# Three regroupings in a two-stage kernel: an earlier half of w_out, groups that share a wait, products moved ahead of block 2

## The chip, the cores and the metric

The kernel runs on one core of a Trainium2 chip. The metric is the device time of one execution in microseconds. The median of seven executions counts, and less is better.

## The reference

The first half is a normalised linear attention over 8 batches of 8 heads, 576 rows and 64 columns. The second half is a two-layer network with a leaky activation over all 4608 rows.

```python
kv  = einsum('bhsd,bhse->bhde', k, v)          # per head, 64 x 64
out = einsum('bhsd,bhde->bhse', q, kv)
x   = out / sqrt(mean(out*out, -1) + 1e-6) * g_norm
x   = x.transpose(0, 2, 1, 3).reshape(4608, 512)
h   = x @ w_in                                 # 512 -> 2048
g   = maximum(h, 0) + alpha * minimum(h, 0)
y   = g @ w_out                                # 2048 -> 512, float32
```

## The kernel before

The 4608 rows are cut into nine blocks (`w` = 0 to 8) of 512. For each block the first layer makes 16 groups (`g`) of 128 features. A group is four matmuls (`m1_mm`), one for each of four pairs of heads, which sum into one PSUM bank. `m1_evac` then empties that bank: ScalarE writes `m_sb`, and VectorE makes `gt` out of `m_sb` and the bank. The second layer is the y products (`y_mm`): each of the four row tiles (`a`) of a block sums 16 products, one per group, into a bank, and `y_out` copies that bank and stores it. A product reads `gt` of its group and one 128-row block of `w_out`.

Nothing is scheduled by the compiler. All five engines run in the order in which the code issues to them (`manual_schedule`), so a line of code that is moved is moved on every queue that it issues to. The eight PSUM banks are named by pools: `H_POOL` (h0 to h2), `ps_s` ("s"), `ps_y` ("y") and `ps_o` (o0 to o2). A new tile of a name waits until the last reader of the old one is done.

Loads from memory are issued by GpSimd, on one queue, in the order of the code. `load_rest` (L190) issues the four quarters of `w_in`, two quarters of `w_out`, then k, q and v of batch 1, then the other two quarters of `w_out` (L197). Each `load` is two transfers. Transposes by DMA and the stores of results are issued on the queue of SyncE (SP).

Blocks 0 and 1 take their input from batches 0 and 1 by way of TensorE: `step_t` transposes q, `step_kv` makes kv of the batch, `step_ot` multiplies both for a pair and ends with a square on ScalarE (or VectorE), `ssq_mm` sums the squares by a matmul and takes Ln and Exp on ScalarE, and `norm` writes the input `xt` of that pair on VectorE. For block 1 these steps stand between the y products of block 0, which `ahead` issues by hand, one group of four tiles at a time (`ya` to `yd`, L623 to L668). `ssq_mm` of all four pairs of block 1 uses the bank "s" (`S_POOL`). The regroup of batch 2's q, a VectorE copy, stands between the norms of pairs 2 and 3; behind it SP issues the transpose that makes `qtm`.

From block 2 on the input `xm` comes another way. `tile_a` multiplies a tile of rows and squares it, `tile_b` and `tile_c` make its scale, `tile_d` writes the scaled rows, and SP transposes them into `xm`. `phase_steps` lays these out as steps, one per group of the block before. The rows that are left over of batch 1 come by `step_tail_ot`, `step_tail_ssq` and `tail_norm`.

In the main loop (L676) each group of block `w` is followed by y products. In block 1 they are block 1's own, of tile 0, two groups behind; later blocks issue those of the block before, and block 2 also what is left of block 1. Two small copies on GpSimd (`gate`) hold the loads of batch 3 back: the first waits for `qtm` of batch 2, the second for `xm` of block 2.

Of the kernel before, what the change touches and what calls it, by code (L numbers as in the profile page):

```python
# [9 lines left out]
FP32 = mybir.dt.float32  # L10
FP16 = mybir.dt.float16
# [6 lines left out]
def kernel(  # L18
# [14 lines left out]
    N_TOK, D_MODEL = out.shape  # L33
    D_FF = moe_w_in.shape[1]

    P = 128
    NPAIR = H // 2
    W = 512
    NW = N_TOK // W
    TPW = W // P  # L40
# [4 lines left out]
    NF = D_FF // P  # L45
    NC = D_MODEL // P
    assert NC == NPAIR and 0 < REM < P
    inv_d = 1.0 / D
    NB_PE = 2

    const_p = ctx.enter_context(tc.tile_pool(name="constp", bufs=1))
    w_p = ctx.enter_context(tc.tile_pool(name="weights", bufs=1))
# [20 lines left out]
            name=nc.get_next_instruction_name(),  # L73
# [33 lines left out]
    def load(b, nm, h0=0, h1=H):  # L107
        load_part(b, nm, True, h0, h1)
        load_part(b, nm, False, h0, h1)
# [50 lines left out]
    WQ = 4  # L160
    w_in_sb = []
    w_out_sb = []
    FW = D_FF // WQ
    GW = NF // WQ
# [6 lines left out]
        )  # L171
        w_in_sb.append(t)

    def load_w_out(i):
        t = w_p.tile([P, GW, D_MODEL], FP16, name=f"w_out_sb{i}")
        nc.gpsimd.dma_start(
            out=t[:],
            in_=moe_w_out[i * GW * P : (i + 1) * GW * P, :].rearrange("(g p) m -> p g m", p=P),
        )
        w_out_sb.append(t)  # L180

    def w_in_blk(c, g):
        i, r = divmod(g, GW)
        return w_in_sb[i][:, c, r * P : (r + 1) * P]

    def w_out_blk(g):
        i, r = divmod(g, GW)
        return w_out_sb[i][:, r, :]

    def load_rest():  # L190
        for i in range(WQ):
            load_w_in(i)
        load_w_out(0)
        load_w_out(1)
        for nm in "kqv":
            load(1, nm)
        for i in range(2, WQ):  # L197
            load_w_out(i)


    warm_ps = ps_y.tile([P, W], FP32, name="warm_ps", tag="y")
# [209 lines left out]
    def tile_b(b, t):  # L411
        n, _, sq = tiles[b, t]
        ss = attn_p.tile([P, H], FP32, name="ss", bufs=3)
        nc.vector.tensor_reduce(  # L414
            out=ss[0:n], in_=sq[0:n], op=ALU.add, axis=mybir.AxisListType.X,
        )
        tiles[b, t][2] = ss
# [14 lines left out]
    def tile_d(b, t):  # L432
        n, ot_ps, rg = tiles.pop((b, t))
        x = attn_p.tile([P, H, D], FP16, name="xrow", bufs=3)
        nc.vector.tensor_mul(out=x[0:n], in0=ot_ps[0:n], in1=rg[0:n])  # L435
        i = 0
        while i < n:
            w, c = divmod(b * S + t * P + i, W)
            m = min(n - i, W - c)
            nc.sync.dma_start_transpose(  # L440
                out=xm(w)[:, :, c : c + m], in_=x[i : i + m].rearrange("p h d -> p (h d)"),
            )
            i += m

    def phase_steps(w):


        if w >= NW:
            return []
        todo = [(b, t) for b in range(NB_PE, min(B, w + 1)) for t in range(NT)  # L450
                if (b, t) not in done and b * S + t * P < (w + 1) * W]
        done.update(todo)
        steps = []

        kv_at = {NB_PE: 3, NB_PE + 1: 6, NB_PE + 2: 2}.get(w, 0)
        n = {NB_PE: 4, NB_PE + 1: 2}.get(w, 0)
        steps += [([], [], []) for i in range(n)]

        lags = (0, 1, 4) if w == NB_PE else (0, 1, 2)
        if w == NB_PE:  # L460
            todo = [x for t in todo for x in (t, None)][:-1]
        if w in (NB_PE + 1, NB_PE + 2):
            k = [b for b, t in todo].index(w)
            todo[k:k] = [None] * (3 if w == NB_PE + 1 else 1)
        for i in range(len(todo) + lags[2]):
            a, b, d = (
                [todo[i - k]] if 0 <= i - k < len(todo) and todo[i - k] else [] for k in lags
            )
            begin = [lambda x=x: tile_b(*x) for x in b] + [lambda x=x: tile_d(*x) for x in d]
            mid = [lambda x=x: tile_c(*x) for x in b]  # L470
            end = [lambda x=x: tile_a(*x) for x in a]
            steps.append((begin, mid, end))
        if w < B:
            steps[kv_at][2 if w == NB_PE else 1].append(lambda: step_kv(w, pool=next_o() if kv_at else (ps_s, "s")))
        return steps
# [5 lines left out]
    H_POOL = [(ps_h, f"h{i}") for i in range(3)]  # L481

    def m1_mm(h_ps, w, g, cs, cols=slice(0, W)):
        for c in cs:
            nc.tensor.matmul(  # L485
                out=h_ps[:, cols], lhsT=w_in_blk(c, g), rhs=xt_of(w, c)[:, cols],
                start=(c == 0), stop=(c == NC - 1 and cols.stop == W),
            )
# [13 lines left out]
    def m1_group(w, g, pool=None):  # L502
        if pool is None:
            pool = H_POOL[n_group[0] % 3]
            n_group[0] += 1
        h_ps = pool[0].tile([P, W], FP32, name="h_ps", tag=pool[1])
        m1_mm(h_ps, w, g, range(NC))
        m1_evac(h_ps, w, g)


    def y_mm(y, w, a, g, cols=slice(0, D_MODEL)):
        nc.tensor.matmul(  # L512
            out=y[:], lhsT=gts[w, g][:, a * P : (a + 1) * P], rhs=w_out_blk(g)[:, cols],
            start=(g == 0), stop=(g == NF - 1),
        )
# [107 lines left out]
    def ahead(g0, g1, tiles=range(TPW)):  # L623
        for g in range(g0, g1):
            for a in tiles:
                y_mm(ys[a], 0, a, g)
# [3 lines left out]
    QW = NF - GW  # L630
    regroup(1, "k")
    ahead(0, 3)
    regroup(1, "q")
    ahead(3, 6)
    step_t(1, 0, S_POOL)
    step_t(1, 1, O1, nc.scalar)
    step_t(1, 2, H_POOL[0])
    step_t(1, 3, H_POOL[1], nc.scalar)
    ahead(6, 7)
    step_kv(1, pool=S_POOL)  # L640
    ahead(7, 8)
    step_ot(1, 0, H_POOL[0])
    step_ot(1, 1, O1)
    step_ot(1, 2, H_POOL[1], nc.vector)
    ahead(8, 9, range(2))
    ssq_mm(1, 0, S_POOL)
    ahead(8, 9, range(2, TPW))
    ahead(9, 10)
    ssq_mm(1, 1, S_POOL)
    norm(1, 0)  # L650
    ahead(10, 11)
    step_ot(1, 3, H_POOL[0])
    norm(1, 1)
    ssq_mm(1, 2, S_POOL)
    ahead(11, QW)
    ahead(QW, NF, (0,))
    ssq_mm(1, 3, S_POOL)
    norm(1, 2)
    regroup(2, "q")
    transpose_q(2)  # L660
    y_out(ys[0], 0, 0)
    ahead(QW, NF, (1,))
    norm(1, 3)
    ahead(QW, NF, (2,))
    y_out(ys[1], 0, 1, nc.vector)
# [6 lines left out]

    LOAD_G = 6
    n_group[0] = 1
    AHEAD = NF - 2
    for w in range(1, NW):  # L676
        steps = phase_steps(w + 1)
        for g in range(NF):
            if g == LOAD_G and 4 < w + 2 < B:
                load_batch(w + 2)  # L680
            if w == 1:
                parts = [(0, g - NF + AHEAD)] if g >= NF - AHEAD else []
            else:
                n0 = AHEAD if w == 2 else 0

                n1, d = TPW * NF - n0, 2 * (w == 2)
                cut = lambda i: max(0, (n1 + d) * i // NF - d)
                parts = [divmod(n0 + i, NF) for i in range(cut(g), cut(g + 1))]
            begin, mid, end = steps.pop(0) if steps else ([], [], [])
            for f in begin:  # L690
                f()
            m1_group(w, g, [H_POOL[1], S_POOL, H_POOL[2], H_POOL[0]][g % 4] if w == 1 else None)
            for f in mid:
                f()
            for a, gg in parts:
                if gg == 0:
                    pool, tag = ((ps_y, "y"), (ps_s, "s"))[a % 2]
                    y = pool.tile([P, W], FP32, name="y_ps", tag=tag)
                wy = w if w == 1 else w - 1
                y_mm(y, wy, a, gg)  # L700
                if gg == NF - 1:
                    y_out(y, wy, a)
            for f in end:
                f()
            if (w, g) == (1, 9):
                step_tail_ot(0, next_o())
            if (w, g) == (1, 11):
                step_tail_ssq(0, next_o())
            if (w, g) == (1, 13):
                tail_norm(0)  # L710
            if (w, g) == (1, 0):
                regroup(2, "k", eng=nc.gpsimd)
            if (w, g) == (1, 2):


                gate = const_p.tile([1, 1], FP16, name="gate")
                nc.gpsimd.tensor_copy(out=gate[:], in_=qtms[2][0:1, 0, 0:1])
                load(3, "q")
                load(3, "k")
            if (w, g) == (1, 9):  # L720
                regroup(3, "q", eng=nc.gpsimd)
            if (w, g) == (1, 12):

                nc.gpsimd.tensor_copy(out=gate[:], in_=xm(2)[0:1, 0, W - 1 : W])
                load(3, "v")
                transpose_q(3)
                regroup(3, "k", eng=nc.gpsimd)
            for i in {5: (0, 1), 6: (2, 3), 7: (4,), 8: (5,)}.get(g, ()) if w == 2 else ():
                load_part(4, "qkv"[i // 2], i % 2 == 0)
            if w > 1 and g == LOAD_G + 3 + 3 * (w == 2) and w + 2 < B:  # L730
                regroup_batch(w + 2)
            if w > 1 and g == NF - 3 and w + 2 < B:
                transpose_q(w + 2)
# [43 lines left out]
```

## Time and profile before

| | |
|---|---|
| median of 7 executions | 291.58 us (291.37 to 291.88) |
| profiled execution | 291.47 us, span 289.5 us |
| TensorE matmul busy | 280.7 us (97% of the span), 1545 matmuls |
| TensorE weight load busy | 138.6 us (48%) |
| VectorE busy | 165.8 us (57%) |
| ScalarE busy | 154.4 us (53%) |
| GpSimd busy | 99.2 us (34%) |
| mean DMA rate | 123 GB/s |

The profiled execution's time is 2.0 us more than its span. A row of the profile names the engine, the line of the kernel, what is written and read, the shape and the count, then busy time and mean duration. Engines are PE (TensorE matmul), PEld (its weight loads), DVE (VectorE), ACT (ScalarE), POOL (GpSimd) and SP (SyncE). Matmuls overlap: a row gives the latency of each, while PE takes the next one after a shorter step, which can be read from two start times.

### The profile page before, as it was taken

The page shows a single profiled execution, that of the slowest core. Times are in us where ns is not written, and L with a number is a line of the kernel's source. Part 1 is how long each engine was busy: PE and PEld are TensorE (multiplying, and loading weights), DVE is VectorE, ACT ScalarE, POOL GpSimd, SP SyncE. Part 2 cuts the span into 40 slices and gives each one's busy share as a digit, 9 for nine tenths or more (in the row PEclk, how much of TensorE's full clock was granted, in tenths as well). Part 3 has the DMA queues.
Part 4 walks back from the last instruction along what each step waited for, and adds up shares of the span by engine and source line. Part 5 has one row for each costly group of instructions (what it writes and reads, how often), then busy time and mean ns, then how long its engine had stood idle before and what let it go on. Part 6 is the DMA issues. An engine that isn't in the chain of part 4 may idle for free.

```text
span 289.5 us, 4268 instructions
## 1 busy us (share of the span) xinstructions
PE 280.7 (97%) x1545; PEld 138.6 (48%) x1545; DVE 165.8 (57%) x256; ACT 154.4 (53%) x300; POOL 99.2 (34%) x109
## 2 busy tenths in 40 slices
PE   5899999999999999999999999999999999999994
PEld 1544464554454554455445544554445444444443
DVE  4448846698777576448744864478448644444300
ACT  1298438587665664448543844486448544444220
POOL 8822330555658237504842474243004100000000
PEclk9999999999999999999999999999999999999999
DMA  7999999999899837971899189815212312121133
GB/s 90 198 206 206 198 204 198 187 210 169 137 154 180 177 65 98 208 178 39 122 207 199 30 132 209 163 31 93 45 36 57 82 38 48 45 47 43 39 72 72
DMA packets 66196, 35.54 MB, mean 123 GB/s; under 512 B 32752, under 2 KB 61696, under 8 KB 66176
## 3 DMA queue, kind: packets, MB, share of 16 engines
q0 software_dynamic: 29632, 18.35, 45.3%
q1 hardware_dynamic: 36384, 16.80, 29.1%
q8 instruction: 12, 0.20, 0.3%
q10 hardware_dynamic: 160, 0.13, 0.2%
q14 instruction: 8, 0.07, 0.1%
HBM read 36.71 MB, written 9.44 MB: 159 GB/s over the span
## 4 chain that ended last, share of the span: by engine, by line
PE 93%; DMA 2%; ACT 2%; DVE 1%; issue 0%; POOL 0%; POOLq 0%; DVEq 0%
PE h_ps L485 42%; PE y_ps L512 38%; PE kv_ps L246 3%; PE otm_ps L402 2%; DMA qst<-in_q_dram 2%; PE yc L512 1%; PE ya L512 1%; PE yb L512 1%; PE yd L512 1%; PE qt_ps L222 1%; ACT sq_sb L268 0%; PE ot_ps L279 0%; ACT rstd L297 0%; ACT rstd L300 0%; PE ssq_ps L295 0%
## 5 line engine op out<-in xcount | busy, mean ns | idle before, releaser
L494 DVE SCALAR_TENSOR_TENSOR gt<-m_sb,beta_sb,h_ps 128x512 f16<-128x512 f32 x144 | 105.7, 744 | 74.8 <-ACT m_sb L492 74.2
L512 PE MATMUL y_ps<-w_out_sb,gt 128*128 128x512 f16 (+1 forms) x528 | 131.1, 373 | 0.0
L492 ACT ACTIVATE m_sb<-h_ps 128x512 f32<-128x512 f32 x144 | 85.6, 597 | 83.2 <-PE h_ps L485 82.1
L485 PE MATMUL h_ps<-xm,w_in_sb 128*128 128x512 f16 x448 | 115.0, 379 | 0.0
L512 PEld LDWEIGHTS <-gt 128*128 128x128 f16 x592 | 57.6, 98 | 65.1 <-DVE gt L494 0.5
L485 PEld LDWEIGHTS <-w_in_sb 128*128 128x128 f16 x584 | 55.7, 98 | 60.5 <-issue 1.9
L426 POOL TENSOR_TENSOR rg<-ss,g_all 128x512 f32<-128x512 f32 (+1 forms) x30 | 31.3, 1042 | 77.9 <-ACT ss L424 72.3
L485 PE MATMUL h_ps<-xt,w_in_sb 128*128 128x512 f16 (+1 forms) x136 | 30.7, 366 | 0.1
L522 ACT COPY y_sb<-y_ps 128x512 f32<-128x512 f32 (+1 forms) x32 | 18.4, 576 | 16.1 <-PE y_ps L512 15.9
L414 DVE TENSOR_REDUCE ss<-sqm_sb 128x8 f32<-128x512 f32 (+1 forms) x30 | 20.5, 682 | 8.6 <-ACT sqm_sb L408 8.4
L435 DVE TENSOR_TENSOR xrow<-otm_ps,rg 128x512 f16<-128x512 f32 (+1 forms) x30 | 20.5, 682 | 3.7 <-POOL rg L426 3.7
L408 ACT ACTIVATE sqm_sb<-otm_ps 128x512 f32<-128x512 f32 (+1 forms) x30 | 17.8, 592 | 6.6 <-PE otm_ps L402 6.6
L112 POOL COPY ksb<-kst 128x2560 f16<-128x2560 f16 x6 | 14.0, 2327 | 15.9 <-DMA kst<-in_k_dram 15.9
L112 POOL COPY qsb<-qst 128x2560 f16<-128x2560 f16 x5 | 11.6, 2317 | 9.0 <-issue 9.0
L402 PEld LDWEIGHTS <-qtm 128*128 128x128 f16 x120 | 9.2, 98 | 7.1
L402 PE MATMUL otm_ps<-kv_sb,qtm 128*128 128x128 f16 x120 | 11.6, 219 | 0.0
L246 PEld LDWEIGHTS <-ksb 128*128 128x128 f16 x160 | 9.7, 98 | 2.6 <-issue 0.6
L421 ACT ACTIVATE ss<-ss,eps_t 128x8 f32<-128x8 f32 (+1 forms) x30 | 9.0, 301 | 2.8 <-DVE ss L414 2.5
L205 PE MATMUL warm_ps<-warm,mask 128*128 128x512 f16 x19 | 7.3, 527 | 3.3 <-DVE eps_t L147 3.3
L246 PE MATMUL kv_ps<-vst,ksb 128*128 128x128 f16 x160 | 10.4, 219 | 0.0
L232 ACT COPY qt_sb<-qt_ps 128x576 f16<-128x576 f16 x4 | 2.5, 639 | 13.3 <-PE qt_ps L222 13.3
L250 DVE TENSOR_TENSOR kv_sb<-kv_ps,mask 128x512 f16<-128x512 f32 (+1 forms) x9 | 5.6, 627 | 5.2 <-PE kv_ps L246 5.2
(76 smaller groups left out, 130.6 us busy)
## 6 DMA issues: line engine op xcount, KB each, us to landing
out_dram<-y_sb SPq DMA_DIRECT2D x70, 128.0 KB, 2.4
qst<-in_q_dram POOLq DMA_DIRECT2D x8, 320.0 KB, 4.9
kst<-in_k_dram POOLq DMA_DIRECT2D x7, 320.0 KB, 8.6
vst<-in_v_dram POOLq DMA_DIRECT2D x7, 320.0 KB, 10.4
qst<-in_q_dram POOLq DMA_DIRECT2D x8, 256.0 KB, 6.4
w_in_sb<-in_moe_w_in_dram POOLq DMA_DIRECT2D x4, 512.0 KB, 10.0
w_out_sb<-in_moe_w_out_dram POOLq DMA_DIRECT2D x4, 512.0 KB, 14.6
kst<-in_k_dram POOLq DMA_DIRECT2D x7, 256.0 KB, 9.8
```

The costliest lines, as they stand in the source:

```text
L112: (eng or nc.vector).tensor_copy(out=bufs[b % NBUF][nm][:, :, h0:h1, :].rearrange("p t h d -> p h t d"), in_=stages[b % NBUF][nm][:, h0:h1],)
L246: nc.tensor.matmul(out=kv_ps[:, j - j0, :], lhsT=ks(t), rhs=vs(t), start=(t == 0), stop=(t == NT - 1),)
L402: nc.tensor.matmul(out=ot_ps[:, 2 * j : 2 * j + 2, :], lhsT=qtms[b][:, t * NPAIR + j, :], rhs=kvs[b, j], start=True, stop=True,)
L408: nc.scalar.activation(out=sq[0:n], in_=ot_ps[0:n], func=AF.Square)
L414: nc.vector.tensor_reduce(out=ss[0:n], in_=sq[0:n], op=ALU.add, axis=mybir.AxisListType.X,)
L426: nc.gpsimd.tensor_tensor(out=rg[0:n], in0=ss[0:n].unsqueeze(2).to_broadcast([n, H, D]), in1=g_all[0:n].unsqueeze(1).to_broadcast([n, H, D ...
L435: nc.vector.tensor_mul(out=x[0:n], in0=ot_ps[0:n], in1=rg[0:n])
L485: nc.tensor.matmul(out=h_ps[:, cols], lhsT=w_in_blk(c, g), rhs=xt_of(w, c)[:, cols], start=(c == 0), stop=(c == NC - 1 and cols.stop == W),)
L492: nc.scalar.activation(out=m_sb[:], in_=h_ps[:], func=AF.Relu, scale=-1.0)
L494: nc.vector.scalar_tensor_tensor(out=gt[:], in0=m_sb[:], scalar=beta_sb[:, g : g + 1], in1=h_ps[:], op0=ALU.mult, op1=ALU.add,)
L512: nc.tensor.matmul(out=y[:], lhsT=gts[w, g][:, a * P : (a + 1) * P], rhs=w_out_blk(g)[:, cols], start=(g == 0), stop=(g == NF - 1),)
L522: nc.scalar.copy(out=y_sb[:, cols], in_=y[:])
```

## The change

There are three parts. `load_w_out` takes a range of groups, and the third quarter of `w_out` is loaded as two halves, the first ahead of v of batch 1. The by-hand order of block 0's products and block 1's input steps is shifted accordingly: more products ahead of the transposes, kv and the first ssq, fewer between the later ssq steps. In block 1 the first three groups issue their first three products each and then their fourths. At block 1's last group, five products of its second tile are issued, and block 2 issues the rest; the last `tile_d` for block 2 comes one group earlier, the tail's steps one group later, and the second gate one group earlier.

```diff
+    def load_w_out(g0, g1):
+        t = w_p.tile([P, g1 - g0, D_MODEL], FP16, name=f"w_out_sb{g0}")
...
     def load_rest():
         for i in range(WQ):
             load_w_in(i)
-        load_w_out(0)
-        load_w_out(1)
-        for nm in "kqv":
-            load(1, nm)
-        for i in range(2, WQ):
-            load_w_out(i)
+        load_w_out(0, GW)
+        load_w_out(GW, 2 * GW)
+        load(1, "k")
+        load(1, "q")
+        load_w_out(2 * GW, 2 * GW + GW // 2)
+        load(1, "v")
+        load_w_out(2 * GW + GW // 2, 3 * GW)
+        load_w_out(3 * GW, NF)
...
+            if w == NB_PE and i >= len(todo) + lags[2] - 2:
+                d = [todo[-1]] if i == len(todo) + lags[2] - 2 else []
...
     regroup(1, "q")
-    ahead(3, 6)
+    ahead(3, 7)
     step_t(1, 0, S_POOL)
     step_t(1, 1, O1, nc.scalar)
     step_t(1, 2, H_POOL[0])
     step_t(1, 3, H_POOL[1], nc.scalar)
-    ahead(6, 7)
+    ahead(7, 9)
     step_kv(1, pool=S_POOL)
-    ahead(7, 8)
+    ahead(9, 10)
     step_ot(1, 0, H_POOL[0])
     step_ot(1, 1, O1)
     step_ot(1, 2, H_POOL[1], nc.vector)
-    ahead(8, 9, range(2))
+    ahead(10, 11, range(2))
     ssq_mm(1, 0, S_POOL)
-    ahead(8, 9, range(2, TPW))
-    ahead(9, 10)
+    ahead(10, 11, range(2, TPW))
+    ahead(11, QW)
     ssq_mm(1, 1, S_POOL)
     norm(1, 0)
-    ahead(10, 11)
+    ahead(QW, NF, (0,))
     step_ot(1, 3, H_POOL[0])
     norm(1, 1)
     ssq_mm(1, 2, S_POOL)
-    ahead(11, QW)
-    ahead(QW, NF, (0,))
+    ahead(QW, NF, (1,))
     ssq_mm(1, 3, S_POOL)
     norm(1, 2)
     regroup(2, "q")
     transpose_q(2)
     y_out(ys[0], 0, 0)
-    ahead(QW, NF, (1,))
     norm(1, 3)
     ahead(QW, NF, (2,))
...
+    AHEAD1 = 5
...
                 parts = [(0, g - NF + AHEAD)] if g >= NF - AHEAD else []
+                parts += [(1, i) for i in range(AHEAD1)] if g == NF - 1 else []
...
+                todo = [(a, gg) for a in range(TPW) for gg in range(NF)]
+                if w == 2:
+                    todo = todo[AHEAD:NF] + todo[NF + AHEAD1 :]
...
-            m1_group(w, g, [H_POOL[1], S_POOL, H_POOL[2], H_POOL[0]][g % 4] if w == 1 else None)
+            if (w, g) == (1, 0):
+                hs = [pool.tile([P, W], FP32, name="h_ps", tag=tag)
+                      for pool, tag in (H_POOL[1], S_POOL, H_POOL[2])]
+                for i, h_ps in enumerate(hs):
+                    m1_mm(h_ps, w, i, range(NC - 1))
+                for i, h_ps in enumerate(hs):
+                    m1_mm(h_ps, w, i, (NC - 1,))
+                    m1_evac(h_ps, w, i)
+            elif w == 1 and g > 2:
+                m1_group(w, g, [H_POOL[1], S_POOL, H_POOL[2], H_POOL[0]][g % 4])
+            elif w > 1:
+                m1_group(w, g)
...
-            if (w, g) == (1, 9):
+            if (w, g) == (1, 10):
                 step_tail_ot(0, next_o())
-            if (w, g) == (1, 11):
+            if (w, g) == (1, 12):
                 step_tail_ssq(0, next_o())
...
-            if (w, g) == (1, 12):
+            if (w, g) == (1, 11):
                 nc.gpsimd.tensor_copy(out=gate[:], in_=xm(2)[0:1, 0, W - 1 : W])
                 load(3, "v")
```

More of the change, by code (lines that the diff above doesn't have):

```diff
@@ L172, in load_w_in @@
         w_in_sb.append(t)
-    def load_w_out(i):
-        t = w_p.tile([P, GW, D_MODEL], FP16, name=f"w_out_sb{i}")
+    def load_w_out(g0, g1):
+        t = w_p.tile([P, g1 - g0, D_MODEL], FP16, name=f"w_out_sb{g0}")
         nc.gpsimd.dma_start(
             out=t[:],
-            in_=moe_w_out[i * GW * P : (i + 1) * GW * P, :].rearrange("(g p) m -> p g m", p=P),
+            in_=moe_w_out[g0 * P : g1 * P, :].rearrange("(g p) m -> p g m", p=P),
         )
-        w_out_sb.append(t)
+        w_out_sb.extend(t[:, r, :] for r in range(g1 - g0))
     def w_in_blk(c, g):
@@ L186, in w_out_blk @@
     def w_out_blk(g):
-        i, r = divmod(g, GW)
-        return w_out_sb[i][:, r, :]
+        return w_out_sb[g]
     def load_rest():
@@ L674 @@
     n_group[0] = 1
+    y_open = {}
     AHEAD = NF - 2
+    AHEAD1 = 5
     for w in range(1, NW):
@@ L682 @@
                 parts = [(0, g - NF + AHEAD)] if g >= NF - AHEAD else []
+                parts += [(1, i) for i in range(AHEAD1)] if g == NF - 1 else []
             else:
                 n0 = AHEAD if w == 2 else 0
-                n1, d = TPW * NF - n0, 2 * (w == 2)
+                todo = [(a, gg) for a in range(TPW) for gg in range(NF)]
+                if w == 2:
+                    todo = todo[AHEAD:NF] + todo[NF + AHEAD1 :]
+                n1, d = len(todo), 2 * (w == 2)
                 cut = lambda i: max(0, (n1 + d) * i // NF - d)
-                parts = [divmod(n0 + i, NF) for i in range(cut(g), cut(g + 1))]
+                parts = todo[cut(g) : cut(g + 1)]
             begin, mid, end = steps.pop(0) if steps else ([], [], [])
@@ L697 @@
                     pool, tag = ((ps_y, "y"), (ps_s, "s"))[a % 2]
-                    y = pool.tile([P, W], FP32, name="y_ps", tag=tag)
+                    y_open[a] = pool.tile([P, W], FP32, name="y_ps", tag=tag)
                 wy = w if w == 1 else w - 1
-                y_mm(y, wy, a, gg)
+                y_mm(y_open[a], wy, a, gg)
                 if gg == NF - 1:
-                    y_out(y, wy, a)
+                    y_out(y_open.pop(a), wy, a)
             for f in end:
                 f()
-            if (w, g) == (1, 9):
+            if (w, g) == (1, 10):
                 step_tail_ot(0, next_o())
-            if (w, g) == (1, 11):
+            if (w, g) == (1, 12):
                 step_tail_ssq(0, next_o())
```

## The prediction

> **What bounds the kernel now.** I read the page first: its busy line and the chain that ended last.
>
> ```profile
> PE 280.7 (97%) x1545; PEld 138.6 (48%) x1545; DVE 165.8 (57%) x256; ACT 154.4 (53%) x300; POOL 99.2 (34%) x109
> ...
> PE 93%; DMA 2%; ACT 2%; DVE 1%; issue 0%; POOL 0%; POOLq 0%; DVEq 0%
> ```
>
> TensorE (PE) is 93% of the chain. Then PE's waits, all of them:
>
> ```profile
> PE warm_ps L205 <- DVE eps_t L147: 3.3, 1, 3.3
> PE qt_ps L222 <- DVE qsb L112: 0.8, 1, 0.8
> PE ssq_ps L328 <- ACT sq_sb L268: 0.3, 1, 0.3
> ```
>
> All three end before 18.2 us, in code that the change leaves alone. Then PE's timeline (start, duration, line) over the changed stretch:
>
> ```profile
> 44.16 0.38 PE L295 MATMUL ssq_ps<-sq_sb,mask 128*128 128x512 f16 x1
> 44.38 0.38 PE L512 MATMUL ya<-w_out_sb,gt 128*128 128x512 f16 x1
> ...
> 45.26 0.39 PE L279 MATMUL ot_ps<-qt_sb,kv_sb 128*128 128x64 f16 x2
> 45.48 0.38 PE L295 MATMUL ssq_ps<-sq_sb,mask 128*128 128x512 f16 x1
> ...
> 47.43 0.38 PE L295 MATMUL ssq_ps<-sq_sb,mask 128*128 128x512 f16 x1
> ...
> 50.23 2.75 PE L485 MATMUL h_ps<-xt,w_in_sb 128*128 128x512 f16 x12
> 52.82 0.38 PE L512 MATMUL y_ps<-w_out_sb,gt 128*128 128x512 f16 x1
> ```
>
> One product costs PE 0.216 us (44.38 less 44.16); the 0.38 is latency. Block 1's first twelve products run from 50.23 without a pause (12 x 0.216 = 2.59, and the next starts at 52.82): the wait for the last pair, which groups 0 to 2 are to share, is not paid here. I compared all start-to-start steps after 21 us: 0.216 for 512 columns, but for a stray 0.016 us and one place, the entry of block 2, 0.34 apart:
>
> ```profile
> 69.08 0.38 PE L512 MATMUL y_ps<-w_out_sb,gt 128*128 128x512 f16 x1
> 69.42 1.02 PE L485 MATMUL h_ps<-xm,w_in_sb 128*128 128x512 f16 x4
> ```
>
> So PE has 0.12 us to give back in the changed code, and whatever is made to wait in it moves the end. Last, what PE's neighbours do, ScalarE (ACT) and VectorE (DVE):
>
> ```profile
> 44.58 0.69 ACT L297 ACTIVATE rstd<-ssq_ps,eps_t 128x512 f32<-128x512 f32 x1 [0.16 <-PE ssq_ps L295]
> 45.30 0.63 ACT L300 ACTIVATE rstd<-rstd 128x512 f32<-128x512 f32 x1
> 45.83 0.58 ACT L268 ACTIVATE sq_sb<-ot_ps 128x512 f16<-128x512 f32 x1
> 46.31 0.68 ACT L297 ACTIVATE rstd<-ssq_ps,eps_t 128x512 f32<-128x512 f32 x1
> ...
> 51.30 0.60 ACT L492 ACTIVATE m_sb<-h_ps 128x512 f32<-128x512 f32 x1 [0.28 <-PE h_ps L485]
> ```
>
> ```profile
> 49.23 0.75 DVE L306 SCALAR_TENSOR_TENSOR xt<-ot_ps,g2col,rstd 128x512 f16<-128x512 f32 x1
> ...
> 51.93 2.47 DVE L494 SCALAR_TENSOR_TENSOR gt<-m_sb,beta_sb,h_ps 128x512 f16<-128x512 f32 x3 [1.35 <-ACT m_sb L492]
> ```
>
> The last pair's xt ends at 49.98 (49.23 + 0.75) and is first read by the fourth product of block 1, at 50.23 + 3 x 0.216 = 50.88: 0.90 us in hand. Group 0's gt ends at 51.93 + 0.74 = 52.67, just 0.15 us ahead of its reader at 52.82.
>
> **The loads.** By the landing records the queue gives 512 KB in 2.53 us (the last two w_out quarters land at 41.49 and 44.02), so the half piece takes 1.27. v of batch 1 lands at 40.2 instead of 38.93; w_out blocks 8 and 9 land at 37.2, 10 and 11 at 41.5, the rest at 44.0 as before. PE's needs move too: eight more products stand ahead of kv, which goes from 39.52 to 39.52 + 8 x 0.216 = 41.25, so v has 1.05 in hand, where it had 0.59. Block 8 is read at 40.4, block 10 at 43.9, block 12 at 46.1: all landed. The extra issue on POOL (0.76, the row of the third quarter) lies in a queue that is full until 52.99; POOL's next work, k's regroup at 50.10, waits for the same bytes. Cost nothing; with the cover gone, v would cost its lateness, 1.27 at most.
>
> **The order before block 1.** No product is added, so the moves are free unless a chain gets less cover. Up to ssq of pair 1 every pair of neighbours keeps its cover, eight products (1.73 us) later: 44.16 becomes 45.89. But between ssq of pair 1 and ssq of pair 3 stood twelve products and now stand eight: 47.43 - 44.16 = 3.27 becomes 3.27 - 4 x 0.216 = 2.41. ssq of pairs 2 and 3 use the same bank (S_POOL), free when ACT's Ln of pair 2 has ended: 46.31 + 0.68 - 44.16 = 2.83 after ssq of pair 1. That chain is ACT's own (Ln, Exp, Square, Ln back to back), so it doesn't shrink. With 0.05 us for the release (the Square that ended PE's wait at 18.14 ended at 18.09) PE stalls 2.88 - 2.41 = **0.47 us**. Bounds: 0.3, if both Ln were as quick as the 0.60 of the m_sb row, to 0.6, without the 0.1 by which the Square overlaps the Exp (0.47 is taken: it is these very four rows). Queued behind are the last eight products and block 1.
>
> **The shared wait.** Groups 0 to 2 do their first three products each, then the fourths. Group 0's last product moves from the fourth place to the tenth: 50.23 + 9 x 0.216, 6 x 0.216 = 1.30 us later. From that product's start to gt's end took 52.67 - 50.88 = 1.79, with 0.05 for the release 1.84. The first y product still stands thirteenth and reads gt of group 0; counted from the block's start it can go at 1.94 + 1.84 = 3.78, PE is there at 2.59: a stall of **1.19 us**. Bounds 1.0 to 1.4, one product's step either way. Behind it wait group 3 and all later matmuls. The later y products don't stall: gt of group 1 comes one DVE step (0.66) after group 0's, its reader 1.08 after. What the sharing buys, 6 x 0.216 of cover for the last pair, was worth 0: 0.90 was in hand. In the new order the pair is later (Ln, Exp, q's regroup and two norms still stand before it), but ends by my count about 2.9 us after its ssq, when the tenth product stands at 3.9; unshared, it would have cost about 0.3.
>
> Here a rule bears on it. Row: at 17.8 PE stood 0.35 us at ssq (L328) while six h_ps products stood behind it, and none passed. The Trainium skill, "TensorE: Matmul & The Clock Gate", Part 3, says that weight loads may be pulled ahead but matmuls start and end strictly in order. By it group 3's four products can't fill the hole; could they, the stall would be 1.19 - 4 x 0.216 = 0.33, and the time 292.2.
>
> **Block 1's end.** Five products of the second tile go ahead of block 2 (1.08 us of cover), and the last tile_d one group earlier. The 0.12 us goes (bounds 0 to 0.12, no more is there). The tail's ssq, a group later, still ends ahead: its norm (68.43 to 69.17 now) keeps its place behind group 13's gt, and block 2 starts at 72. Behind the stalls the gated loads of batch 3 follow q's regroup, 1.73 later (qtm lands at 55.37 + 1.73 = 57.1, read at 56.31 + 0.47 + 1.19 = 57.97); xm, landed at 69.28, comes at about 71.0, needed at 69.3 + 1.66 + 1.08 = 72.0. Block 2's 45 instead of 50 products are the same five. They change SP's order once: the last two transposes of batch 3's rows, issued at 91.04 and landed 4.03 later for a read at 96.25, now stand behind an output pair (two issues of 0.6). At worst xm of block 3 comes at 91.04 + 1.54 + 1.2 + 4.03 = 97.8, when PE gets there (96.25 + 1.54): cost 0, with the cover used up at that bound.
>
> **Sum.** 0.47 + 1.19 - 0.12 = +1.54. The profiled execution took 291.47 (span 289.5), giving 293.01; the median of the seven is 0.11 above it: **293.1 us**. By bounds +1.18 (0.3 + 1.0 - 0.12) to +2.0 (0.6 + 1.4): 292.8 to 293.6. The granted clock is 1.00 in every stretch that I asked, 36 to 80 us, and the 0.35 us idle left no mark on it. The same page, Part 1, puts the drop to half clock after an idle window of some 3.4 us, which two pauses under 1.3 us don't fill; if it did drop for one window, an estimate by the page is 1.7 us more.
>
> **Rivals.** *Only the y stall shows* (0.06): ACT's chain is tighter than the rows. For it: ssq of pair 3 had 0.4 us in hand before. 291.58 + 1.07 = 292.65. *A later arrival adds to it* (0.07): qtm has 0.87 in hand, xm 1.0, and xm's transposes took 2.3 to 7.9 us from issue to landing; one that takes 1.5 longer than counted costs 0.5 to 0.6 there: 293.7. *Not slower* (0.05): the shared wait pays in runs that the profile doesn't show. The last pair's norm stands on DVE behind q's regroup, which waits for q of batch 2 (landed 46.95, used 48.36). If that landing came 1.41 + 0.90 + 1.54 = 3.9 us later, the old kernel would lose what the new one does, and the time would stay 291.5. Against: the seven times spread over 0.5 us and the profiled one is among them. *Faster* (0.02): PE has no idle time to give.
>
> The forecast itself has 0.80. The range 292.5 to 293.8 takes in the first two rivals. A measurement tells 0.2% (0.58 us) from no change: faster 0.02, same 0.05, slower 0.93.
>
> **What would show it.** In the new profile PE should wait about 0.5 us before the ssq (L296) of pair 3, the last ahead of block 1's twelve products, and about 1.2 before the first y product after them (L516, released by DVE gt); the step into block 2 should be 0.216, and kv of batch 1 should start near 41.25 without a wait. I am wrong if PE runs through the thirteenth product, or if v, qtm or xm appear among its waits.

## The result and the profile after

| | before | after |
|---|---|---|
| median | 291.67 us (42 executions) | 292.64 us (17 executions) |
| ratio | | 1.0033, 95% interval 1.0024 to 1.0042 |
| profiled execution | 291.47, span 289.5 | 292.65, span 290.5 |

The changed kernel is slower by 0.97 us by the medians (0.33%). Its 292.64 us is inside the predicted range, but the difference is about 0.6 less than the predicted 1.54. Both stalls that were predicted are there. These are PE's waits in the profile after (us in total, times, longest; a wait counts from where the last matmul's latency has ended; of the two for vst one is batch 0's, ahead of the changed code):

```profile
PE y_ps L516 <- DVE gt L498: 1.0, 1, 1.0
...
PE kv_ps L247 <- DMA vst<-in_v_dram: 0.7, 2, 0.4
...
PE ssq_ps L296 <- ACT rstd L298: 0.3, 1, 0.3
```

In PE's timeline after, over the stretch shown of before, the same rows stand with holes between them:

```profile
46.63 0.38 PE L296 MATMUL ssq_ps<-sq_sb,mask 128*128 128x512 f16 x1
46.84 1.03 PE L516 MATMUL yb<-w_out_sb,gt 128*128 128x512 f16 x4
48.18 0.38 PE L296 MATMUL ssq_ps<-sq_sb,mask 128*128 128x512 f16 x1 [0.31 <-ACT rstd L298]
...
50.12 2.75 PE L489 MATMUL h_ps<-xt,w_in_sb 128*128 128x512 f16 x12
53.92 0.39 PE L516 MATMUL y_ps<-w_out_sb,gt 128*128 128x512 f16 x1 [1.04 <-DVE gt L498]
...
70.61 1.03 PE L516 MATMUL y_ps<-w_out_sb,gt 128*128 128x512 f16 x4
71.48 1.24 PE L489 MATMUL h_ps<-xm,w_in_sb 128*128 128x512 f16 x5
```

Below, a hole is the time from the end of a product's step of 0.216 to the next start; it is 0.17 more than the wait in square brackets, which counts from the end of the latency of 0.38. The four yb products take 0.86, so ssq of pair 3 could have gone at 47.70; it went at 48.18, 0.48 late. Block 1's twelve products end their steps at 52.71; the y product goes at 53.92, 1.21 late. Block 2 is entered at 71.48 without a hole. The releasers in the same profile, ACT and DVE:

```profile
47.45 0.68 ACT L298 ACTIVATE rstd<-ssq_ps,eps_t 128x512 f32<-128x512 f32 x1
```

```profile
50.23 0.74 DVE L307 SCALAR_TENSOR_TENSOR xt<-ot_ps,g2col,rstd 128x512 f16<-128x512 f32 x1
...
53.11 2.07 DVE L498 SCALAR_TENSOR_TENSOR gt<-m_sb,beta_sb,h_ps 128x512 f16<-128x512 f32 x3 [1.54 <-ACT m_sb L496]
```

The Ln of pair 2 ends at 48.13 and frees the bank for 48.18. Group 0's gt ends near 53.85 and frees the y product for 53.92.

One thing differs that no edit touches. The full clock was granted 7.8 us into this execution, and 12.2 us into that of before (the clock records of the two traces). The first row below is from PE's timeline of before, the second from that of after: the same twenty transposes, ahead of all changed code.

```profile
8.48 2.32 PE L222 MATMUL qt_ps<-ident,qsb 128*128 128x128 f16 x20 [0.80 <-DVE qsb L112]
```

```profile
8.05 1.29 PE L223 MATMUL qt_ps<-ident,qsb 128*128 128x128 f16 x20 [0.37 <-DVE qsb L112]
```

So PE reached the first ya product at 31.15 here and at 32.36 there. The two profiles may not be subtracted without allowing for this 1.2 us. With it they balance: from the first ya product on, the holes after are 0.11 and 0.50 (transposes and kv of batch 1, which wait for q and v), 0.48 and 1.21, and before there is only the 0.12 at block 2's entry; 2.30 - 0.12 - 1.21 = 0.97, and the spans differ by 1.0.

### The profile page after: what moved, and what is told of

It is laid out like the page before. It is cut to its first block, busy times and chain, and to the rows that moved or that the text cites. A ratio compares the mean times of both kernels' runs of the same rounds, so it can differ in the third digit from the quotient of the medians.

```text
span 290.5 us, 4269 instructions
## 1 busy us (share of the span) xinstructions
PE 279.5 (96%) x1545; PEld 137.0 (47%) x1545; DVE 165.5 (57%) x256; ACT 153.8 (53%) x300; POOL 99.7 (34%) x110
## 4 chain that ended last, share of the span: by engine, by line
PE 83%; DMA 12%; POOL 2%; ACT 1%; issue 0%; DVE 0%; POOLq 0%; DVEq 0%
PE y_ps L516 38%; PE h_ps L489 38%; DMA w_out_sb<-in_moe_w_out_dram 5%; DMA vst<-in_v_dram 5%; PE kv_ps L247 3%; PE otm_ps L403 2%; DMA kst<-in_k_dram 2%; POOL w_in_sb L168 1%; PE yd L516 1%; PE yc L516 1%; ACT rstd L298 0%; POOL qst L97 0%; PE ssq_ps L296 0%; DVE gt L498 0%; PE ot_ps L280 0%
## 5 line engine op out<-in xcount | busy, mean ns | idle before, releaser
L489 PEld LDWEIGHTS <-w_in_sb 128*128 128x128 f16 x584 | 55.6, 98 | 60.6 <-DMA w_in_sb<-in_moe_w_in_dram 1.6
```

The lines of the kernel that those rows point to most:

```text
L489: nc.tensor.matmul(out=h_ps[:, cols], lhsT=w_in_blk(c, g), rhs=xt_of(w, c)[:, cols], start=(c == 0), stop=(c == NC - 1 and cols.stop == W),)
```

## The experiments

Each was timed in 5 rounds against the kernel before on the same chip, but for the second profile of before; ratios are to that. L numbers are those of the kernel at hand.

**Block 1's groups one after the other again** (the changed kernel without the sharing):

```diff
-            if (w, g) == (1, 0):
-                hs = [...]        # three groups, their fourth products last
-            elif w == 1 and g > 2:
+            if w == 1:
                 m1_group(w, g, [H_POOL[1], S_POOL, H_POOL[2], H_POOL[0]][g % 4])
```

> The changed kernel with block 1's first three groups issued one after the other again. My theory (PE has no idle time, so each stall adds itself to the end): the 1.21 us wait of the first y product goes, and the fourth product of block 1 waits about 0.25 us for the last pair's xt (it ended at 50.97, the product would stand at 50.77): 292.64 - 1.21 + 0.25 = 291.7 us. Rival (the y wait only moves, to a later reader of gt): no change, 292.6 us.

Measured 291.45 us, ratio 0.9987 (0.9976 to 0.9998). The y wait is gone from the profile and the fourth product of block 1 waits 0.25 us. PE's timeline has block 1's twelve products (3.00, the 0.25 included, where the changed kernel has 2.75) and the first y product right behind them:

```profile
49.54 3.00 PE L489 MATMUL h_ps<-xt,w_in_sb 128*128 128x512 f16 x12
52.38 0.38 PE L516 MATMUL y_ps<-w_out_sb,gt 128*128 128x512 f16 x1
```

The rival falls. The time came out 0.25 lower than my figure. Without the sharing the other parts are a small gain. Its profile also has holes of 0.15 and 0.32 at the entries of blocks 2 and 3.

**Another bank for ssq of pair 3:**

```diff
-    ssq_mm(1, 3, S_POOL)
+    ssq_mm(1, 3, O1)
```

> The changed kernel with the ssq of pair 3 in bank o1 instead of the bank that pair 2's ssq holds. My theory: its wait of 0.48 us goes and nothing takes its place, since the tenth product of block 1 would stand at 51.58 and xt of the last pair ends at 50.97: 292.64 - 0.48 = 292.2 us, the y wait stays at 1.2. Rival (ScalarE is the bound there, so what is won comes back as a longer y wait): 292.6 us, y wait 1.7.

Measured 292.43 us, ratio 1.0021 (1.0008 to 1.0034). The wait shrank from 0.48 to 0.20 and did not go: in PE's timeline ssq of pair 3 starts at 47.53, with its four products' steps over at 47.33:

```profile
46.46 1.03 PE L516 MATMUL yb<-w_out_sb,gt 128*128 128x512 f16 x4
47.53 0.39 PE L296 MATMUL ssq_ps<-sq_sb,mask 128*128 128x512 f16 x1
```

The new bank, o1, holds pair 1's product until that pair's norm on DVE has ended, which I had overlooked. DVE's timeline of the same kernel:

```profile
46.72 0.75 DVE L307 SCALAR_TENSOR_TENSOR xt<-ot_ps,g2col,rstd 128x512 f16<-128x512 f32 x1 [0.76 <-ACT rstd L301]
```

It ends at 47.47 and PE goes 0.06 later. The y wait stayed at 1.20, so the rival's longer wait didn't come. The shorter wait is shown; that the time fell by 0.2 is not, since the interval overlaps that of the changed kernel (1.0024 to 1.0042).

**The first y product one group later:**

```diff
+                parts = {2: [], 3: [(0, 0), (0, 1)]}.get(g, parts)
```

> The changed kernel with the first y product of block 1 one group later, behind group 3 together with the second; the groups go on sharing. My theory: group 3's four products (0.86 us) fill most of the 1.21 us; the y product then waits 0.34 at most: 292.64 - 0.87 = 291.8 us. Rival (groups 3 and 4 then wait for their banks, so the hole only moves): 292.6 us.

Measured 292.09 us, ratio 1.0008 (0.9998 to 1.0019). PE's timeline shows the 0.34 that was expected, and one more hole of 0.44:

```profile
53.47 0.39 PE L516 MATMUL y_ps<-w_out_sb,gt 128*128 128x512 f16 x1 [0.18 <-DVE gt L498]
54.13 0.39 PE L516 MATMUL y_ps<-w_out_sb,gt 128*128 128x512 f16 x1 [0.27 <-DVE gt L498]
```

The second y product now follows the first at once, but its gt comes one DVE step (0.66) later. The rival's waits of groups 3 and 4 for their banks are not there. The same execution, which at 293.08 is one of the two longest of twelve, also has a hole of 1.39 for xm at block 3's entry. Group 3's four products fill part of the hole when they are put ahead of the y product. They didn't do so by themselves in the changed kernel, where they stood behind it until 54.15 (53.92 plus its step): this agrees with the strict order of matmuls that the Trainium skill gives in "TensorE: Matmul & The Clock Gate", Part 3.

**Both of these:**

> The changed kernel with both edits: y product one group later and pair 3's ssq in bank o1. My theory: the two savings add: 292.64 - 0.87 - 0.48 = 291.3 us, 0.1% below the kernel before (291.67). Rival (the loads ahead of block 1 set the pace, and PE only waits for them instead): 291.7 us or more, with waits for v or q in the profile.

Measured 291.57 us, ratio 0.9999 (0.9987 to 1.0010): no different from before. The holes of the two kernels stand side by side in its profile (0.20, 0.34, 0.44), so the savings add up; the two waits that I had missed (0.20 and 0.44) take part of them back. A hole of 0.31 for xm stands at block 3's entry. The rival's waits for q or v after the first ya product aren't there in this execution.

**The sharing alone**, added to the kernel before (the `hs` lines of the change and nothing else):

> The kernel before with the shared wait of block 1's first three groups alone. My theory: the y product waits 1.2 us and nothing is bought: 291.67 + 1.2 = 292.9 us, more than the whole change. Rival (the last pair's xt is late in executions that start sooner than the profiled one did, and the sharing covers that): 291.7 to 292.3 us.

Measured 292.00 us, ratio 1.0011 (1.0002 to 1.0019). This was the surprise. The y wait is there in full, 1.20 us, and costs 0.3. PE's timeline shows the hole, and the entry of block 2:

```profile
53.67 0.39 PE L512 MATMUL y_ps<-w_out_sb,gt 128*128 128x512 f16 x1 [1.04 <-DVE gt L494]
...
69.93 0.38 PE L512 MATMUL y_ps<-w_out_sb,gt 128*128 128x512 f16 x1
70.21 0.59 PE L485 MATMUL h_ps<-xm,w_in_sb 128*128 128x512 f16 x2
```

My rival had the size right for a wrong reason: the last pair is not late. The sharing costs 1.2 us in the changed kernel (292.64 against 291.45) and 0.3 here, so something further on takes the stall up.

**The kernel before once more**, for a second profile:

> The kernel before once more, for a second profile. My theory: PE gapless after 21 us again, but for the entry of block 2. Rival (the profile shown had a late start): where the full clock is granted sooner than 12.2 us, PE comes sooner to the transposes and kv of batch 1 and waits there for q and v, up to 1.3 us, and the end stays near 291.6 us.

One execution, 292.09 us. It started early (first ya product at 31.14) and shows what takes the stall up. From PE's waits and timeline:

```profile
PE h_ps L485 <- DMA xm<-xrow: 1.4, 1, 1.4
```

```profile
68.24 0.38 PE L512 MATMUL y_ps<-w_out_sb,gt 128*128 128x512 f16 x1
70.00 0.59 PE L485 MATMUL h_ps<-xm,w_in_sb 128*128 128x512 f16 x2 [1.39 <-DMA xm<-xrow]
```

The hole at block 2's entry is 70.00 - 68.24 - 0.216 = 1.54 us here and 0.12 in the profile that I predicted from. Only 0.35 was lost at kv. So the rival was right about a hidden wait, and named the wrong one.

**The loads and the by-hand order alone** (no sharing, block 1's end as before):

> The kernel before with the loads and the by-hand order of the change alone (no sharing, block 1's end as before). My theory as predicted: +0.47 from the shared ssq bank, +0.25 from the last pair: 291.67 + 0.7 = 292.4 us. Rival, from the changed kernel's profile, where PE came to kv 1.2 us sooner than in the profile of before and still waited 0.5 us for v: in such executions the kernel before waits for q and v by 1.3 us more, so the new order of loads gains about what the bank costs: 291.7 us.

Measured 291.92 us, ratio 1.0019 (1.0002 to 1.0037; two of twelve executions at 294 widen it). The profile has both predicted stalls, 0.47 at the bank and 0.25 at the last pair, and then 0.75 at block 2's entry. By the medians (291.71 before) the cost is 0.2. It falls between theory and rival and decides little by itself.

**Block 1's end alone** (five products, tile_d a group earlier, tail and gate moved):

> The kernel before with block 1's end of the change alone (five products ahead of block 2, last tile_d a group earlier). My theory: the wait at block 2's entry goes, 0.12 us in the profile of before: 291.55 us. Rival (that wait is longer in other executions, since xm lands behind the loads of batch 3): 291.1 us.

Measured 291.19 us, ratio 0.9981 (0.9971 to 0.9991). The rival is right: the part is worth 0.5 us, four times the 0.12 that I had given it. A new hole of 0.88 for xm stands at block 3's entry in its profile (the third y product starts at 95.55):

```profile
95.12 0.81 PE L514 MATMUL y_ps<-w_out_sb,gt 128*128 128x512 f16 x3
96.64 0.60 PE L487 MATMUL h_ps<-xm,w_in_sb 128*128 128x512 f16 x2 [0.71 <-DMA xm<-xrow]
```

A table from six of the traces (when PE could enter block 2, when the last transpose for xm was issued and landed, when k of batch 3 had landed) gave the new theory:

| kernel | PE ready | xm issued | xm landed | k landed | hole |
|---|---|---|---|---|---|
| before | 69.29 | 66.83 | 69.28 | 67.94 | 0.12 |
| before, second profile | 68.45 | 65.99 | 69.87 | 68.75 | 1.54 |
| sharing alone | 70.15 | 67.69 | 70.08 | 68.13 | 0.06 |
| loads alone | 68.86 | 66.40 | 69.48 | 68.18 | 0.75 |
| end alone | 69.71 | 65.13 | 69.88 | 68.97 | 0.30 |
| after | 71.48 | 67.80 | 70.26 | 68.41 | 0 |

PE's arrival moves by 3 us and the issue by 2.7, but xm lands within a microsecond, 0.9 to 2.0 behind k of batch 3. The theory overlooks the issue column: in the three rows issued at 66.83 or later (before, sharing alone, after) xm lands 2.39 to 2.46 after its own issue, so there the issue may have set the landing, and not k (in the row before both fit).

**Sharing and end together**, without the loads:

> The kernel before with the sharing and block 1's end, without the loads and the by-hand order. My new theory (the loads of batch 3 fix when xm of block 2 lands, 69.3 to 70.3 in all profiles so far, so a stall of PE ahead of it is paid only as far as PE gets there after it): the y stall of 1.2 and the five products' cover of 1.08 take up the same wait, so the gain of the end alone (0.55) is mostly not there: 291.7 + 1.2 less a wait of 0.9 = 292.0 us, and no wait at block 2's entry. Rival (each part adds its own figure: +0.32 for the sharing, -0.55 for the end): 291.5 us.

Measured 292.36 us, ratio 1.0019 (1.0009 to 1.0030), with no hole at block 2's entry (PE ready at 71.11, xm landed at 69.66). The parts don't add: 0.3 and -0.5 make +0.6. Two edits drew on one wait: with block 1's end in, the sharing costs 292.36 - 291.19 = 1.17, the whole stall, as it does in the changed kernel. The theory's figure was 0.36 too low, the rival's 0.9. The 0.36 stays open: xm here landed 2.45 after its issue at 67.21, not behind k, and the profiled execution, at 292.30, took as long as that of the sharing alone (292.29).

**k of batch 3 behind the second gate**, in the kernel before:

```diff
                 load(3, "q")
-                load(3, "k")
...
+                load(3, "k")
                 load(3, "v")
```

> The kernel before with k of batch 3 loaded behind the second gate, after xm of block 2, instead of behind q; nothing else moved. My new theory (xm lands about a microsecond after that k, whatever PE and SP did): xm lands 2.4 us after its issue at 66 to 67, so at 68.4 to 69.2, the wait at block 2's entry (0.12 and 1.55 in the two profiles) goes to 0.3 or less, and the time to about 290.9 us if kv of batch 3 is not late for its k; if it is, its wait stands in the profile at about 79.6 and the time says nothing. Rival (xm is late by its own chain of rows): the wait at block 2's entry stays, 291.7 us.

With no load in flight (q of batch 3 landed at 64.69) the last transpose, issued at 66.15, lands at 68.55, 2.4 us later, the earliest of all, and PE's timeline runs into block 2 nearly without a hole (0.07) although this execution started early, at 30.79:

```profile
68.40 0.38 PE L512 MATMUL y_ps<-w_out_sb,gt 128*128 128x512 f16 x1
68.69 1.02 PE L485 MATMUL h_ps<-xm,w_in_sb 128*128 128x512 f16 x4
```

With k ahead of it, a transpose issued about as early landed 3.88 and 3.08 later (65.99 in the second profile of before, 66.40 with the loads alone). So where the transpose is issued this early, the loads of batch 3 hold xm back; for a later issue see the part on why the prediction was right. The time, 294.97 us (ratio 1.0115), says nothing, as was allowed for: kv of batch 3 then waits 2.04 for its inputs, and xm of block 3 another 2.09.

**End alone, one output pair handed over later:**

```diff
-                if gg == NF - 1:
+                if gg == NF - 1 and (w, a) == (2, 2):
+                    late = [lambda y=y_open.pop(a): y_out(y, 1, 2)]   # run in the next group
+                elif gg == NF - 1:
```

> The kernel before with block 1's end alone, and the output of block 1's third tile handed over one group later, so that SP has the last two transposes of block 3's xm ahead of that output pair, as the kernel before has them. With the end alone xm of block 3 was late by 0.88 us in the profile. My theory: the pair's place costs up to 1.2 us of issue there, the wait at block 3's entry falls to 0.3 or less, and the time to 290.8 us. Rival (xm of block 3 is late because the loads of batch 4 end late): the wait stays at 0.3 to 0.9 and the time at 291.2 us.

Measured 290.91 us, ratio 0.9975 (0.9965 to 0.9985): faster than the kernel before and than the changed one. SP's timeline with the end alone, then with the pair behind:

```profile
90.39 1.18 SPq L532 DMA_DIRECT2D out_dram<-y_sb  x2
91.67 2.51 SPq L439 DMA_TRANSPOSE xm<-xrow  x2
```

```profile
86.92 6.19 SPq L439 DMA_TRANSPOSE xm<-xrow  x4
93.20 1.18 SPq L532 DMA_DIRECT2D out_dram<-y_sb  x2
```

The hole at block 3's entry went from 0.88 to 0. That does not shut out the rival: v of batch 4, the last load ahead, also landed 0.96 sooner (94.20 instead of 95.16). The traces part the two. The third of the four transposes, for which PE waited with the end alone, lands 1.43 to 1.57 behind that v in the seven profiles with the output pair ahead of it, and 0.75 to 0.94 in the five with the pair behind (the run with k moved apart). So the pair costs about 0.6 us, and the rest of the 1.57 by which this transpose came sooner (95.03 instead of 96.60) went with the loads. The two intervals of the time overlap, so that the 0.3 us between these two kernels comes from this edit is not shown.

## Why the prediction was right, and where it was wrong

- **What bounds the kernel.** Right for the profile it was read from, too strong as a general statement. "PE has 0.12 us to give back" holds where PE starts late. In the second profile of before PE stood 1.9 us in all after 21 us. (The profile it was read from has one more hole after 21 us, 0.21 at 21.99, ahead of the changed code.)
- **The loads.** v was put at 40.2, the blocks at 37.2, 41.5 and 44.0; they landed at 40.53, 37.71, 41.09 and 44.18. "Cost nothing" failed in the profiled execution: PE came to kv at 40.16, a microsecond sooner than 41.25, because of its early start, and stood 0.50 there: v among the waits, one of the signs of being wrong that I had named. An early start meets the old order in the same place: the transposes and kv of batch 1 lost 0.37 in the second profile of before and 0.54 to 1.02 in the five other runs with its order, against 0 to 0.68 in the six with the new one. So it isn't a cost of the change.
- **The shared bank.** 0.47 predicted, 0.48 measured, by the chain that was named.
- **The shared wait.** 1.19 predicted, 1.21 measured. That it buys little also held: unshared, the last pair costs 0.25, where 0.3 was put.
- **Block 1's end, the step that was mis-sized.** "The 0.12 us goes (bounds 0 to 0.12, no more is there)" took one execution's hole for the kernel's. Alone the part gained 0.5 us, and the second profile of before had a hole of 1.54. By the medians it is worth 0.5 also on top of the loads and the order (291.92 against 291.45). With the stalls at 0.48 + 1.21 = 1.69, the measured 0.97 leaves about 0.7 for this term and whatever the loads gain; that remainder was not measured by itself.
- **What stands behind it**: "qtm lands at 55.37 + 1.73 = 57.1", and "xm comes at about 71.0". qtm was issued 1.14 later than before and landed at 55.32, not later at all; xm landed at 70.26. I let these landings follow PE and DVE. For qtm that is wrong: it lands at 55.0 to 55.6 in all profiles, whatever its issue (48.39 to 50.34), and so the gate opens and batch 3 is loaded at almost fixed times. For xm it is half right. Of the twelve profiles with k in its place, seven issued the last transpose at 65.13 to 66.40, and it landed 0.91 to 1.46 behind k; five issued it at 66.83 to 67.80, and it landed 2.39 to 2.46 after its issue, as with k moved (2.40). So it comes with its issue or with the loads, whichever is later. In the profile after it was issued 0.97 later than before and landed 0.98 later, 1.85 behind k: with its issue, as I had predicted. That it wasn't 1.7 later is mostly the early start: 0.11 + 0.50 + 0.48 + 1.21 - 1.21 = 1.09.
- **Rivals.** "Only the y stall shows" had the measured time, 292.65 against 292.64, by luck: the stall at ssq, which it left out, is there with 0.48, and what it lacked was a gain elsewhere. "A later arrival adds to it" was the wrong sign for block 2. For block 3 the edge that I had named (the output pair on SP) is real, about 0.6 of the lateness behind the 0.88 with the end alone; in the changed kernel's profile PE comes there later than xm (97.24 against 96.96) and has no hole. "Not slower" looked for a hidden wait at the last pair; a hidden wait there was, at xm.
- **The clock.** It stayed granted through the 1.21 us pause: the clock record after has 1.0 from 7.8 us to the end of the work. This agrees with the Trainium skill, "TensorE: Matmul & The Clock Gate", Part 1, which has the clock drop after an idle window of about 3.4 us.

Still open: how often each start occurs, why a transpose held back by k lands now 0.9, now 1.5 us behind it, and the 0.36 of the run with sharing and end together.

## What to carry to other kernels

A stall on the busiest engine is paid in full only if that engine is also the last to arrive at the next join; where a stream of loads sets that join, as in the second profile of before, earlier stalls vanish into it, and edits that draw on the same wait don't add up. So before a hole is priced from a profile, take a second profile of the same kernel: a join where two arrivals lie within a tenth of a microsecond of each other, as at 69.28 and 69.29 here, is a coin toss and not a term. When several groups are made to share a wait, count the first reader of the first group's result: its distance shrinks by everything that was put ahead of the shared step.

## What the runs showed of the hardware

The full clock came between 5.9 us (end alone) and 12.2 us (before) into the span, though the warm-up matmuls start at 3.25 or 3.26 in both. The late grant went with the latest first ya product, 32.36; the others, granted by 9.0, lie between 30.64 and 31.35, where PE waits for w_in instead (0.8 us in the profile after). A DMA transpose of the same size landed 2.4 us after its issue with no loads in flight (66.15 to 68.55, k moved), and up to 7.8 us after it (61.16 to 68.93 in the second profile of before) while batch 3 was loaded.
